# Six experts behind an attention: VectorE's and ScalarE's order written out by hand, the background work dealt into named slots, and the gating's column sums set behind the last group of a step

## The chip, the core and the metric

The kernel runs on one core of a Trainium2 chip. In the profile TensorE is PE (its weight loads PEld), VectorE is DVE, ScalarE is ACT, SyncE is SP, which issues the transfers here. Times are device microseconds (us) unless a unit stands beside them; a kernel's time is the median of its runs.

## The reference: what is computed

An attention with a complex decay per channel (4 batches, 8 heads, 768 positions, width 48 per head) yields 3072 tokens of 384 channels. They go through a mixture of eight experts, each two matrix products with a ReLU between; every token uses every expert, weighted by a gate matrix P that is normalised by rows and columns in turn, eight times.

```
x   = attention(q, k, v, a)                     # [3072, 384]
P   = exp(x @ w_gate - max)                     # [3072, 8]
for _ in range(8):
    P /= P.sum(1, keepdims=True) + 1e-9         # rows
    P /= P.sum(0, keepdims=True) + 1e-9         # columns
    P *= N / E
out = sum over e of P[:, e] * (relu(x @ w1[e]) @ w2[e])     # w1 384x1024, w2 1024x384
```

## The kernel before

**Stages.** `phase1` computes the attention and, beside it, experts 0 and 1, whose results go to DRAM (`ye_d`), as do the tokens (`x_d`). `phase2a` finishes these two experts, prepares the first weights, and does the first three normalising rounds (`HEAD` is 3 of `ITERS` 8). `phase2b`, the stage that the change edits, does experts 2 to 7 and the five other rounds.

**Steps of phase2b.** The 3072 tokens are four units `u` of 768. A step of the loop over `steps` is one unit with one pair of hidden blocks (2 x 128 of the 1024 hidden channels) of one expert. The steps run over two pairs of units (`su`), experts 2 to 7 (`e`), the two units of the pair (`ul`), and four pairs of blocks (`p`): 2 x 6 x 2 x 4 = 96 steps, eight of one expert in a row, called q = 0 to 7 below.

**One step on PE.** The hidden values of a step are four tiles of 128x384: c11, c12, c21, c22 (hidden block by half of the unit's tokens). The kernel makes them by a scheme of the Strassen kind from seven products P1 to P7 with eleven terms. A product's operands are sums of weight blocks (A, S) and of token blocks (B, T). Each operand is split into a high and a low part in fp32r, and each term is three matmuls (high x high, high x low, low x high: L785 to L787), so a step has 33. Two PSUM banks (tag `ph`) serve the products in turn: a product can start once the product before the last has been read. The second layer of a step is issued a step late, among the products of the next one: `l2(k)`, k = 0 to 5, calls `second` for one group of 128 tokens, six matmuls (L746 to L748) into the accumulator `po[k]`; 36 in a step.

**One step on the other engines.** ACT copies P1 and P5 out of PSUM as s1 and s5 (L800). DVE adds (L795): u2 = P6 + s1, u3 = P7 + u2, u4 = u2 + s5, c22 = u3 + s5, c11 = P2 + s1, c21 = P4 + u3, c12 = P3 + u4. Of each c, ACT makes the high part hh of its ReLU (L806), and DVE the remainder hl (L807).

**Background work**, done among the steps:

- Weights: `raw_w` (L648) loads the two weight matrices' blocks of a pair by one transfer of 768 KB, and `prep_w` makes five sums on DVE (L666), copies of the high parts on ACT (L668) and the remainders on DVE (L669) for the tiles wa (A blocks), wb (the sums) and wc (the second matrix).
- Tokens of the next unit: `load_x` (L607) issues the transfers and returns `jobs`: sums on DVE (tx, L623), high copies on ACT (L626) and remainders on DVE (L627) of T1 to T4. `l2` takes up to two jobs per group.
- Normalising: `rows` (five DVE instructions, L593 to L597, the last a partial sum `cs` over tiles), then `columns`: a small matmul by a matrix of ones that finishes the column sums (cp, L601), and four DVE instructions (L602 to L605).
- Ends of an expert: six evictions per unit, by ACT where e = 2 (L753), else by DVE into `oa` (L755), and for e = 7 the transfer to `out` (L757). `start` (L726 to L734), for e = 3, fetches experts 0 and 1 from `ye_d`, scales `oa` by P, and adds them.

**What sets the order.** A schedule is written out by hand for PE alone (L108): PE's order is the order in which the code issues its matmuls. The order on DVE, ACT and SP is chosen by a scheduler with its own estimates of durations, within the program's dependencies; so a background instruction in `l2(1)` may land elsewhere on DVE.

## Time and profile before

| what | value |
|---|---|
| median of three runs | 1807.05 (1807.03 to 1812.23) |
| the profiled execution's own time | 1808.5 |
| its span on the core | 1806.7 |
| its mean granted clock of TensorE | 0.993 |
| second-layer matmuls, lines L746, L747, L748, 1152 each | 385.3, 385.2 and 385.7 busy, 334 to 335 ns each |
| weight loads from DRAM, 48 of 768 KB | 4.2 from issue to landing (median) |

The page's first part gives each engine's busy time and its share of the span. Successive matmuls overlap, so the interval from one's start to the next's is shorter than the 335 ns that one is shown busy. A share is a mean over stages with different limits, so the timeline, the table by stretches and the waits are read for `phase2b` by itself. In a row of the timeline stand the start, the duration, the engine, the line, the operation, output and inputs; a bracket at its end gives idle time before it and what ended this. A line's number is one of the kernel above.

### The profile page before, as it was taken

The page shows a single profiled execution, that of the slowest core. Times are in us where ns is not written, and L with a number is a line of the kernel's source. Part 1 is how long each engine was busy: PE and PEld are TensorE (multiplying, and loading weights), DVE is VectorE, ACT ScalarE, POOL GpSimd, SP SyncE. Part 2 cuts the span into 40 slices and gives each one's busy share as a digit, 9 for nine tenths or more (in the row PEclk, how much of TensorE's full clock was granted, in tenths as well). Part 3 has the DMA queues.
Part 4 walks back from the last instruction along what each step waited for, and adds up shares of the span by engine and source line. Part 5 has one row for each costly group of instructions (what it writes and reads, how often), then busy time and mean ns, then how long its engine had stood idle before and what let it go on. Part 6 is the DMA issues. An engine that isn't in the chain of part 4 may idle for free. (4 is left out here: it accounts for less than half of the span.)

```text
span 1806.7 us, 30538 instructions
## 1 busy us (share of the span) xinstructions
PE 1756.0 (97%) x12024; PEld 1725.3 (95%) x12024; DVE 1361.6 (75%) x3060; ACT 730.1 (40%) x1597; POOL 6.4 (0%) x15
## 2 busy tenths in 40 slices
PE   5989999999999999999999999999999999999998
PEld 3889999999999999999999999999999999999998
DVE  7898999999973778867675757577876767675754
ACT  7544544554543533433343324243433333342421
POOL 1000000000000000000000000000000000000000
PEclk9999999999999999999999999999999999999999
DMA  6333334343442322201010201231220101010100
GB/s 213 94 118 118 109 119 121 119 125 118 120 106 96 122 70 79 97 18 53 18 53 1 71 1 53 84 114 48 88 71 20 52 18 53 11 61 1 53 27 28
DMA packets 120632, 132.83 MB, mean 74 GB/s; under 512 B 9632, under 2 KB 100512, under 8 KB 120480
## 3 DMA queue, kind: packets, MB, share of 16 engines
q1 hardware_dynamic: 119680, 130.41, 23.3%
q8 instruction: 96, 1.57, 0.4%
q14 instruction: 56, 0.46, 0.1%
q10 hardware_dynamic: 800, 0.39, 0.1%
HBM read 88.22 MB, written 23.59 MB: 62 GB/s over the span
## 5 line engine op out<-in xcount | busy, mean ns | idle before, releaser
L748 PE MATMUL po<-wc,hl 128*128 128x384 f32 x1152 | 385.7, 335 | 3.0 <-DVE hl L807 3.0
L746 PE MATMUL po<-wc,hh 128*128 128x384 f32 x1152 | 385.3, 334 | 0.0
L747 PE MATMUL po<-wc,hh 128*128 128x384 f32 x1152 | 385.2, 334 | 0.0
L806 ACT ACTIVATE hh<-c 128x384 fp32r<-128x384 f32 x384 | 200.9, 524 | 322.4 <-DVE c L795 321.1
L807 DVE SCALAR_TENSOR_TENSOR hl<-c,hh 128x384 fp32r<-128x384 f32 x384 | 212.2, 553 | 65.9 <-ACT hh L806 58.0
L748 PEld LDWEIGHTS po<-wc,hl 128*128 128x128 f32 x1152 | 216.5, 188 | 4.3 <-DVE hl L807 4.2
L746 PEld LDWEIGHTS po<-wc,hh 128*128 128x128 f32 x1152 | 216.5, 188 | 0.2 <-ACT hh L806 0.2
L747 PEld LDWEIGHTS po<-wc,hh 128*128 128x128 f32 x1152 | 216.5, 188 | 0.0
L800 ACT ACTIVATE s<-P 128x384 f32<-128x384 f32 x192 | 94.1, 490 | 278.6 <-PE P L787 278.5
L180 PE MATMUL ph<-xl,w 128*128 128x256 f32 x576 | 162.8, 283 | 3.5 <-DVE xl L531 3.4
L185 ACT ACTIVATE hh<-ph 128x256 fp32r<-128x256 f32 x192 | 73.3, 382 | 226.8 <-PE ph L181 226.1
L181 PE MATMUL ph<-xh,w 128*128 128x256 f32 x576 | 162.4, 282 | 0.0
L179 PE MATMUL ph<-xh,w 128*128 128x256 f32 x576 | 162.1, 281 | 0.0
L785 PE MATMUL P<-B,wa 128*128 128x384 f32 x480 | 160.4, 334 | 0.5 <-DVE c L795 0.5
L787 PE MATMUL P<-B,wa 128*128 128x384 f32 x480 | 160.4, 334 | 0.0
L786 PE MATMUL P<-B,wa 128*128 128x384 f32 x480 | 160.4, 334 | 0.0
L158 PE MATMUL po<-w,hh 128*128 128x384 f32 x384 | 136.3, 355 | 0.0
L795 DVE TENSOR_TENSOR c<-P,u 128x384 f32<-128x384 f32 x192 | 106.4, 554 | 31.7 <-PE P L787 30.6
L795 DVE TENSOR_TENSOR u<-u,s 128x384 f32<-128x384 f32 x96 | 53.5, 557 | 100.7 <-ACT s L800 100.3
L159 PE MATMUL po<-w,hh 128*128 128x384 f32 x384 | 129.3, 337 | 0.0
L160 PE MATMUL po<-w,hl 128*128 128x384 f32 x384 | 129.3, 337 | 0.0
L180 PEld LDWEIGHTS ph<-xl,w 128*128 128x128 f32 x576 | 108.9, 189 | 4.4 <-DVE xl L531 4.4
(188 smaller groups left out, 3606.0 us busy)
## 6 DMA issues: line engine op xcount, KB each, us to landing
raw<-in_w_dram SPq DMA_DIRECT2D x48, 768.0 KB, 4.2
qs<-z SPq DMA_DIRECT2D x144, 64.5 KB, 2.6
qk<-in_aqk_dram SPq DMA_DIRECT2D x12, 768.0 KB, 4.7
ks<-kh SPq DMA_DIRECT2D x144, 64.0 KB, 2.6
ye_d<-yst SPq DMA_DIRECT2D x48, 192.0 KB, 1.9
y<-ye_d SPq DMA_DIRECT2D x48, 192.0 KB, 2.4
z<-in_aqk_dram SPq DMA_DIRECT2D x11, 768.0 KB, 7.2
B<-x_d SPq DMA_DIRECT2D x40, 192.0 KB, 3.3
```

What stands on the lines that cost most here:

```text
L179: nc.tensor.matmul(ph, w[:, 0, cs], xh[:, ct, :], start=(ct == 0), stop=False)
L180: nc.tensor.matmul(ph, w[:, 0, cs], xl[:, ct, :], start=False, stop=False)
L181: nc.tensor.matmul(ph, w[:, 1, cs], xh[:, ct, :], start=False, stop=(ct == NCT - 1))
L746: nc.tensor.matmul(po[k], hh[:, s], w2[:, 0, i], start=first, stop=False)
L747: nc.tensor.matmul(po[k], hh[:, s], w2[:, 1, i], start=False, stop=False)
L748: nc.tensor.matmul(po[k], hl[:, s], w2[:, 0, i], start=False, stop=last)
L785: nc.tensor.matmul(ps, t[:, 0, k], x[:, 0], start=first, stop=False)
L786: nc.tensor.matmul(ps, t[:, 0, k], x[:, 1], start=False, stop=False)
L787: nc.tensor.matmul(ps, t[:, 1, k], x[:, 0], start=False, stop=last)
L795: V.tensor_tensor(o, a, b, ALU.add)
L806: A.activation(hh, c, AF.Relu)
L807: V.scalar_tensor_tensor(hl, c, 0.0, hh.bitcast(F32), ALU.max, ALU.subtract)
```

## The change

**Order.** The loop body of `phase2b` becomes a function `step`, run under a manual schedule for DVE and ACT too. Their order is now the order of the code; SP's is still the scheduler's. The first stage and `phase2a` keep the old rule.

**Slots.** A step has six slots, `fill(0)` to `fill(5)`, at fixed places among its instructions, which DVE mostly fills; and `post[0]` and `post[1]`, for copies on ACT. Which background work goes to which slot is set by the step's number n and by q. `deal(k)` runs up to k jobs of `load_x`.

**Weights.** One load of 768 KB becomes two of 384 KB, `raw0` and `raw1` (the two matrices), each issued behind the last reader of its forerunner. `prep_w` becomes `prep_w1` (sums, wa, wb) and `prep_w2` (wc). They run at q = 1, 5, 6, 7 and q = 0, 1, 6, 7, where `prep_w` was called at q = 0 and 5 to 7. `prep_w` itself, still called twice in `phase2a`, makes its copies ahead of its remainders, wb first. Of four preparations issued ahead of step 1 (two in `phase2a`, two in step 0), the third and fourth move to steps 1 and 2.

**PE.** In a step each group `l2(k)` stands one product earlier: P1, l2(0), P6, l2(1), P7, l2(2), P5, l2(3), P2, P4, l2(4), P3, l2(5), where before the sequence was P1, P6, l2(0), P7, l2(1), P5, l2(2), P2, l2(3), P4, l2(4), P3, l2(5).

**Normalising.** `sink` holds steps 4 to 8, where steps 1 to 5 did it. `rows` is in slot 2, `columns` behind `l2(5)`, where they were in `l2(1)` and `l2(4)`.

**Scaling `oa` by P** (e = 2's results) moves from DVE to ACT: for the first two units 12 instructions of their own in steps 10 and 11, for the other two within the eviction itself. The evictions and the adding of experts 0 and 1 (`mixin`) have slots, and the fetch of these two stays ahead by a step.

The core of the diff:

```diff
+        return [
+            tt(t[0], f("B11", 0), f("B11", 1), ALU.add),
+            tt(t[1], t[1], t[4], ALU.add),
+            both(tt(t[0], t[1], t[0]), hi("T1", t[0])),
+            tt(t[2], f("B22", 0), f("B22", 1), ALU.add),
+            both(tt(t[3], t[2], t[0]), hi("T2", t[3])),
+            lo("T1", t[0]),
+            both(tt(t[1], t[2], t[1]), hi("T3", t[1])),
+            lo("T2", t[3]),
+            tt(t[2], f("B21", 0), f("B21", 1), ALU.add),
+            both(tt(t[2], t[2], t[3]), hi("T4", t[2])),
+            lo("T3", t[1]),
+            lo("T4", t[2]),
+        ]
...
+        r = self.raw[j, n] = self.wr.tile([128, 2, C], F32, tag=f"raw{j}", name=f"raw{j}_{n}")
+        self.nc.sync.dma_start(r, src[:, :, j * C:j * C + C])
...
+        def sums():
+            for o, a, b, op in ((0, A21, A22, ALU.add), (1, s[:, 0], A11, ALU.subtract), (2, A11, A21, ALU.subtract), (3, A12, s[:, 1], ALU.subtract), (4, A13, A23, ALU.subtract)):
+                V.tensor_tensor(s[:, o], a, b, op)
+
+        def hi(q):
+            t, k, src = parts[q]
+            return lambda: A.activation(t[:, 0, k], src, AF.Copy)
+
+        def lo(q):
+            t, k, src = parts[q]
+
+            def run():
+                V.tensor_tensor(t[:, 1, k], src, t[:, 0, k].bitcast(F32), ALU.subtract)
+                if q == 1:
+                    self.raw_w(0)
+            return run
+
+        return sums, [hi(q) for q in range(3)], [lo(q) for q in range(3)]
...
+        def lo():
+            V.tensor_tensor(w2[:, 1], raw, w2[:, 0].bitcast(F32), ALU.subtract)
+            self.raw_w(1)
+
+        return lambda: A.activation(w2[:, 0], raw, AF.Copy), lo
...
-                self.raw_w()
+                self.raw_w(0)
+                self.raw_w(1)
                 self.prep_w()
...
+        sink = range(npair, npair + ITERS - HEAD)
...
+            if e == 2:
+                oa[tt] = self.xa.tile([128, C], F32, tag=f"oa{u % SU}_{k}", name=f"oa{tt}")
+                if u < SU:
+                    A.activation(oa[tt], po[k], AF.Copy)
+                else:
+                    A.activation(oa[tt], po[k], AF.Copy, scale=self.P[:, tt, 2:3])
+            else:
+                V.scalar_tensor_tensor(oa[tt], po[k], self.P[:, tt, e:e + 1], oa[tt], ALU.mult, ALU.add)
...
+            def out(k):
+                if done:
+                    slots[(2, 2, 2, 3, 4, 5)[k]].append(lambda: evict(prev, k))
+
+            for k in range(2 * NS):
+                out(k)
+            w2 = q in (0, 6, 7) and n > 0
+            w1 = q in (1, 5, 6, 7) or n == 2
+            if w2 and n > npair and self.nprep[1] < self.nprep[0]:
+                hi, lo = self.prep_w2()
+                post[0].append(hi)
+                slots[1].append(lo)
+            if w1 and self.nprep[0] < len(self.todo):
+                sums, his, los = self.prep_w1()
+                slots[0].append(sums)
+                post[0].extend([his[2], his[0], his[1]])
+                slots[2].extend([los[2], los[0], los[1]])
+                if q in (1, 2):
+                    hi, lo = self.prep_w2()
+                    post[1].append(hi)
+                    slots[3].append(lo)
+            if n in sink:
+                slots[2].append(self.rows)
+            if su == 0 and n == 2 or su and e == 2 and ul == 0 and p == 2:
+                slots[2].append(lambda: deal(3))
+            if e == 2 and ul == 0 and p == 3:
+                slots[0].append(lambda: deal(2))
+                slots[1].append(lambda: deal(1))
+                slots[2].append(lambda: deal(4))
+                slots[3].append(lambda: deal(1))
+                slots[4].append(lambda: deal(1))
+            if su and e == 2 and ul == 0 and p == 2:
+                slots[1].append(lambda: deal(1))
+                slots[3].append(lambda: deal(1))
+            if e == E - 1 and q >= 5:
+                slots[3].append(lambda: deal(1))
+                slots[4].append(lambda: deal(2))
+                slots[5].append(lambda: deal(1))
+            tiles = [(su * SU + k // (2 * NS), k % (2 * NS)) for k in range(4 * NS)]
+            if su == 0 and e == 3 and q in (2, 3):
+                for k in range(2 * NS):
+                    tt = tile_of(q - 2, k)
+                    post[0].append(lambda o=oa[tt], tt=tt: A.activation(o, o, AF.Copy, scale=self.P[:, tt, 2:3]))
+            if 3 <= e < 6 and q in (1, 2):
+                k = (e - 3) * 4 + (q - 1) * 2
+                fetch(*tiles[k])
+                fetch(*tiles[k + 1])
+            if 3 <= e < 6 and q in (2, 3):
+                k = (e - 3) * 4 + (q - 2) * 2
+                slots[2].append(lambda: mixin(*tiles[k]))
+                slots[4].append(lambda: mixin(*tiles[k + 1]))
...
-                if p > 1 or n == 0 or su and e == 2:
-                    for _ in range(min(2, len(jobs))):
-                        jobs.pop(0)()
-                if k == 1 and 0 < n <= ITERS - it:
-                    self.rows()
-                if k == 4 and 0 < n <= ITERS - it:
-                    self.columns(self.psA.tile([128, E], F32, tag="ph", name=f"cp{it + n - 1}"))
 
             s1 = copy("s1", prod("P1", ("A11", "B11")))
+            fill(0)
+            for g in post[0]:
+                g()
+            l2(0)
             u2 = add("u2", prod("P6", ("S2", "T2")), s1)
-            l2(0)
+            l2(1)
+            fill(1)
             u3 = add("u3", prod("P7", ("S3", "T3")), u2)
-            l2(1)
+            l2(2)
+            fill(2)
             s5 = copy("s5", prod("P5", ("S1", "T1"), ("A23", "B32")))
             u4 = add("u4", u2, s5)
             c22 = add("c22", u3, s5)
-            l2(2)
+            h11 = high(1, 1, c22)
+            l2(3)
             c11 = add("c11", prod("P2", ("A12", "B21"), ("A13", "B31")), s1)
-            relu(1, 1, c22)
-            relu(0, 0, c11)
-            l2(3)
+            h00 = high(0, 0, c11)
+            low(1, 1, c22, h11)
             c21 = add("c21", prod("P4", ("A22", "T4"), ("A23", "B31")), u3)
-            relu(1, 0, c21)
+            h10 = high(1, 0, c21)
+            low(0, 0, c11, h00)
+            low(1, 0, c21, h10)
+            for g in post[1]:
+                g()
             l2(4)
+            fill(3)
             c12 = add("c12", prod("P3", ("S4", "B22"), ("S5", "B32")), u4)
-            relu(0, 1, c12)
+            h01 = high(0, 1, c12)
+            fill(4)
+            low(0, 1, c12, h01)
             l2(5)
-            if n == 0:
-                self.prep_w()
-                self.prep_w()
-            if prev is not None and prev[2] == SU - 1:
-                self.prep_w()
-            if e == 3:
-                a = p * 2 if ul == 0 else 8 + p
-                for k in range(a, a + 2 - ul):
-                    start(su * SU + k // (2 * NS), k % (2 * NS))
+            if n in sink:
+                self.columns(self.psA.tile([128, E], F32, tag="ph", name=f"cp{n}"))
+            fill(5)
+
+        with tc.manual_schedule(engines={mybir.EngineType.DVE, mybir.EngineType.Activation}):
...
+            for n, st in enumerate(steps):
+                su, e, ul, p = st
+                if e == 2 and ul == 0 and p == 0:
+                    jobs.extend(self.load_x(xb, 1, su * SU + 1))
+                if e == E - 1 and ul == 1 and p == 0 and su + 1 < SU:
+                    jobs.extend(self.load_x(self.xa, 0, su * SU + 2))
+                step(n, st, steps[n - 1] if n else None)
+            for k in range(2 * NS):
+                second(steps[-1], k)
+                evict(steps[-1], k)
```

Three places in the new order beside the old. First PE at the start of step 1 (P1_1 and P6_1 are products of step 1, po2_0_0 the first group's accumulator, hh and hl the hidden values of step 0). Before:

```order
L785 MATMUL P1_1_8800<-B11_0_8152,wa1_8530 128x384
L786 MATMUL P1_1_8800<-B11_0_8152,wa1_8530 128x384
L787 MATMUL P1_1_8800<-B11_0_8152,wa1_8530 128x384
L785 MATMUL P6_1_8806<-T2_0_8158,wb1_8531 128x384
L786 MATMUL P6_1_8806<-T2_0_8158,wb1_8531 128x384
L787 MATMUL P6_1_8806<-T2_0_8158,wb1_8531 128x384
L746 MATMUL po2_0_0_8812<-wc0_8513,hh00_0_8706 128x384
L747 MATMUL po2_0_0_8812<-wc0_8513,hh00_0_8706 128x384
L748 MATMUL po2_0_0_8812<-wc0_8513,hl00_0_8707 128x384
L746 MATMUL po2_0_0_8812<-wc0_8513,hh10_0_8719 128x384
L747 MATMUL po2_0_0_8812<-wc0_8513,hh10_0_8719 128x384
L748 MATMUL po2_0_0_8812<-wc0_8513,hl10_0_8720 128x384
```

And now:

```order
L894 MATMUL P1_1_8774<-B11_0_8152,wa1_8534 128x384
L895 MATMUL P1_1_8774<-B11_0_8152,wa1_8534 128x384
L896 MATMUL P1_1_8774<-B11_0_8152,wa1_8534 128x384
L798 MATMUL po2_0_0_8788<-wc0_8528,hh00_0_8738 128x384
L799 MATMUL po2_0_0_8788<-wc0_8528,hh00_0_8738 128x384
L800 MATMUL po2_0_0_8788<-wc0_8528,hl00_0_8753 128x384
L798 MATMUL po2_0_0_8788<-wc0_8528,hh10_0_8751 128x384
L799 MATMUL po2_0_0_8788<-wc0_8528,hh10_0_8751 128x384
L800 MATMUL po2_0_0_8788<-wc0_8528,hl10_0_8755 128x384
L894 MATMUL P6_1_8795<-T2_0_8158,wb1_8535 128x384
L895 MATMUL P6_1_8795<-T2_0_8158,wb1_8535 128x384
L896 MATMUL P6_1_8795<-T2_0_8158,wb1_8535 128x384
```

The second-layer group stands between P1 and P6, where it stood behind both.

Second, DVE at the start of step 0 (sum3, wa3, wb3, wc3 are the fourth weight preparation, rs, cs and P_90 the normalising). Before:

```order
L669 TENSOR_TENSOR wa3_8756<-raw3_8753,wa3_8756 128x384
L666 TENSOR_TENSOR sum3_8755<-sum3_8755,raw3_8753 128x128
L669 TENSOR_TENSOR wa3_8756<-raw3_8753,wa3_8756 128x256
L594 TENSOR_SCALAR rs_8344<-rs_8344 128x24
L666 TENSOR_TENSOR sum3_8755<-raw3_8753,sum3_8755 128x128
L595 RECIPROCAL rs_8344<-rs_8344 128x24
L596 TENSOR_TENSOR P_90<-P_90,rs_8344 128x192
L597 TENSOR_REDUCE cs_8345<-P_90 128x8
L669 TENSOR_TENSOR wb3_8757<-sum3_8755,wb3_8757 128x640
L795 TENSOR_TENSOR u2_0_8672<-P6_0_8668,s1_0_8666 128x384
L669 TENSOR_TENSOR wc3_8758<-raw3_8753,wc3_8758 128x768
L795 TENSOR_TENSOR u3_0_8678<-P7_0_8674,u2_0_8672 128x384
```

And now:

```order
L904 TENSOR_TENSOR u2_0_8706<-P6_0_8702,s1_0_8700 128x384
L904 TENSOR_TENSOR u3_0_8712<-P7_0_8708,u2_0_8706 128x384
L904 TENSOR_TENSOR u4_0_8723<-u2_0_8706,s5_0_8721 128x384
L904 TENSOR_TENSOR c22_0_8725<-u3_0_8712,s5_0_8721 128x384
L904 TENSOR_TENSOR c11_0_8736<-P2_0_8729,s1_0_8700 128x384
L919 SCALAR_TENSOR_TENSOR hl11_0_8740<-c22_0_8725,hh11_0_8727 128x384
L904 TENSOR_TENSOR c21_0_8749<-P4_0_8742,u3_0_8712 128x384
L919 SCALAR_TENSOR_TENSOR hl00_0_8753<-c11_0_8736,hh00_0_8738 128x384
L919 SCALAR_TENSOR_TENSOR hl10_0_8755<-c21_0_8749,hh10_0_8751 128x384
```

Preparation and rows are gone from between and ahead of the step's sums, and u2, u3, u4, c22 and c11 follow one another.

Third, DVE in step 49, where the third unit gives way to the fourth (tx and T_3 are `load_x`'s jobs of unit 3). Before:

```order
L795 TENSOR_TENSOR u3_49_14952<-P7_49_14948,u2_49_14937 128x384
L623 TENSOR_TENSOR tx1_3_14911<-tx1_3_14911,tx4_3_14914 128x384
L623 TENSOR_TENSOR tx0_3_14910<-tx1_3_14911,tx0_3_14910 128x384
L623 TENSOR_TENSOR tx3_3_14913<-tx2_3_14912,tx0_3_14910 128x384
L623 TENSOR_TENSOR tx1_3_14911<-tx2_3_14912,tx1_3_14911 128x384
L795 TENSOR_TENSOR u4_49_14972<-u2_49_14937,s5_49_14970 128x384
L795 TENSOR_TENSOR c22_49_14974<-u3_49_14952,s5_49_14970 128x384
L627 TENSOR_TENSOR T1_3_14906<-tx0_3_14910,T1_3_14906 128x384
L666 TENSOR_TENSOR sum28_15517<-raw28_14899 128x128 x3
L623 TENSOR_TENSOR tx2_3_14912<-B21_3_14902 128x384
L627 TENSOR_TENSOR T2_3_14907<-tx3_3_14913,T2_3_14907 128x384
L795 TENSOR_TENSOR c11_49_14992<-P2_49_14985,s1_49_14931 128x384
```

And now:

```order
L904 TENSOR_TENSOR u3_49_15008<-P7_49_15004,u2_49_14995 128x384
L688 TENSOR_TENSOR wb27_14968<-sum27_14966,wb27_14968 128x640
L688 TENSOR_TENSOR wa27_14967<-raw0_27_14732,wa27_14967 128x384
L688 TENSOR_TENSOR wa27_14967<-raw0_27_14732,wa27_14967 128x256
L904 TENSOR_TENSOR u4_49_15031<-u2_49_14995,s5_49_15029 128x384
L904 TENSOR_TENSOR c22_49_15033<-u3_49_15008,s5_49_15029 128x384
L904 TENSOR_TENSOR c11_49_15051<-P2_49_15044,s1_49_14974 128x384
L919 SCALAR_TENSOR_TENSOR hl11_49_15055<-c22_49_15033,hh11_49_15035 128x384
```

Ahead of c11 stood ten background instructions in two places (sum28 is three); now three weight remainders stand between u3 and u4, and none between c22 and c11.

More of the change, by code (lines that the diff above doesn't have):

```diff
@@ L652, in prep_w, with tt, hi, lo @@
-    def prep_w(self):
-        nc, V, A = self.nc, self.nc.vector, self.nc.scalar
-        n = self.nprep
+        def tt(o, a, b, op=ALU.subtract):
+            return lambda: V.tensor_tensor(o, a, b, op)
+        def hi(nm, r):
+            return lambda: A.activation(X[nm][:, 0], r, AF.Copy)
+        def lo(nm, r):
+            return lambda: V.tensor_tensor(X[nm][:, 1], r, f(nm, 0), ALU.subtract)
+        def both(*fs):
+            def run():
+                for g in fs:
+                    g()
+            return run
@@ L675, in phase2a, with prep_w @@
+    def prep_w(self):
+        sums, his, los = self.prep_w1()
+        sums()
+        for q in (2, 0, 1):
+            his[q]()
+        for q in (2, 0, 1):
+            los[q]()
+        for g in self.prep_w2():
+            g()
     def phase2a(self, c2):
@@ L711, in phase2b @@
         tc, nc = self.tc, self.nc
+        V, A = nc.vector, nc.scalar
         self.hp = c2.enter_context(tc.tile_pool(name="hp2", bufs=2))
@@ L714, in phase2b @@
         psD = c2.enter_context(tc.tile_pool(name="psD", bufs=2, space=bass.MemoryType.PSUM))
-        steps = [(su, e, ul, p) for su in range(SU) for e in range(2, E) for ul in range(SU) for p in range(NF // 2)]
         npair = NF // 2
-        po, oa, H = {}, {}, {}
+        NE = E - 2
+        steps = [(su, e, ul, p) for su in range(SU) for e in range(2, E) for ul in range(SU) for p in range(npair)]
+        po, oa, H, Y, jobs = {}, {}, {}, {}, []
+        free = [(pool, tag) for pool, tag in ((self.psC, "po0"), (self.psC, "po1"), (self.psC, "po2"), (psD, "po"), (psD, "po"))]
+        sink = range(npair, npair + ITERS - HEAD)
         def acc(e, u, k):
@@ L739, in second @@
             h, w2 = H[st]
+            w2 = w2[1]
             if p == 0:
@@ L759, in phase2b, with evict @@
-        V, A = nc.vector, nc.scalar
-        jobs, free = [], [(pool, tag) for pool, tag in ((self.psC, "po0"), (self.psC, "po1"), (self.psC, "po2"), (psD, "po"), (psD, "po"))]
-        it = HEAD
-        for n, st in enumerate(steps + [None]):
-            prev = steps[n - 1] if n else None
-            if st is None:
-                for k in range(2 * NS):
-                    second(prev, k)
-                break
+        def evict(st, k):
             su, e, ul, p = st
             u = su * SU + ul
-            if e == 2 and ul == 0 and p == 1:
-                jobs = self.load_x(xb, 1, u + 1)
-            if e == E - 1 and ul == 1 and p == 1 and su + 1 < SU:
-                jobs = self.load_x(self.xa, 0, u + 1)
-            W, w2 = self.W[(su * (E - 2) + e - 2) * npair + p]
-            X = self.X[u]
-            h = {}
-            H[st] = (h, w2)
+            tt = tile_of(u, k)
+            if e == 2:
[6 more added lines that the diff above has]
+                V.scalar_tensor_tensor(oa[tt], po[k], self.P[:, tt, e:e + 1], oa[tt], ALU.mult, ALU.add)
+            if e == E - 1:
+                nc.sync.dma_start(self.out[tt * CH:tt * CH + CH, :], oa[tt])
@@ new lines, in deal, with step, fill @@
+        def deal(k):
+            for _ in range(min(k, len(jobs))):
+                jobs.pop(0)()
+        def step(n, st, prev):
+            su, e, ul, p = st
+            u = su * SU + ul
+            q = ul * npair + p
+            done = prev is not None and prev[3] == npair - 1
+            h = {}
+            H[st] = (h, self.W[(su * NE + e - 2) * npair + p])
+            W, X = H[st][1][0], self.X[u]
+            slots = {k: [] for k in range(6)}
+            post = {k: [] for k in range(3)}
+            def out(k):
[10 more added lines that the diff above has]
+            if w1 and self.nprep[0] < len(self.todo):
+                sums, his, los = self.prep_w1()
+                slots[0].append(sums)
[35 more added lines that the diff above has]
+                slots[4].append(lambda: mixin(*tiles[k + 1]))
+            def fill(k):
+                for g in slots[k]:
+                    g()
@@ L781, in prod @@
                 ps = pool.tile([128, TH], F32, tag=tag, name=f"{nm}_{n}")
-                for q, (wn, xn) in enumerate(terms):
+                for i, (wn, xn) in enumerate(terms):
                     (t, k), x = W[wn], X[xn]
-                    first, last = q == 0, q == len(terms) - 1
+                    first, last = i == 0, i == len(terms) - 1
                     nc.tensor.matmul(ps, t[:, 0, k], x[:, 0], start=first, stop=False)
```

95 lines of the change are left out of this document (38 added, 57 removed).

## The prediction

> Times are microseconds. Step n is pass n of the loop over `steps` (0 to 95); a time "in a step" counts from the issue of its first matmul of P1. q is its place among the eight steps of one expert.
>
> **What bounds the kernel now.** First the busy table of the page: TensorE (PE) is the only full engine.
>
> ```profile
> PE 1756.0 (97%) x12024; PEld 1725.3 (95%) x12024; DVE 1361.6 (75%) x3060; ACT 730.1 (40%) x1597; POOL 6.4 (0%) x15
> ```
>
> The change touches the stage of six experts, so I measure that stage against its own matmuls. From the timeline of PE: the stage's first matmul, its 39th, and its last one.
>
> ```profile
> 632.63 0.33 PE L785 MATMUL P<-B,wa 128*128 128x384 f32 x1
> ...
> 639.22 0.34 PE L787 MATMUL P<-T,wb 128*128 128x384 f32 x1
> ...
> 1800.57 0.34 PE L748 MATMUL po<-wc,hl 128*128 128x384 f32 x1
> ```
>
> Between the first two lie 38 issues: 6.59 / 38 = 0.1734 a matmul. A step has 33 product matmuls (eleven terms of three) and 36 of the second layer; 96 x 69 = 6624 take 1148.6. The stage lasted 1800.57 + 0.17 - 632.63 = 1168.1, so 19.5 are lost. Where, the table by stretches shows (columns: length, then busy time of PE, weight load, DVE, ACT, POOL, then granted clock):
>
> ```profile
> 642.00:644.00 2.00, 1.39 (x6) 1.37 (x6) 0.57 (x2) 0.25 (x1) 0.00 (x0) 0.74 1.13 345
> 644.00:646.00 2.00, 2.00 (x8) 2.00 (x7) 1.71 (x6) 0.00 (x0) 0.00 (x0) 0.50 0.73 205
> ...
> 740.00:764.00 24.00, 22.16 (x126) 21.50 (x125) 18.69 (x40) 7.44 (x15) 0.00 (x0) 1.00 0.34 109
> 764.00:788.00 24.00, 24.00 (x140) 24.00 (x140) 13.58 (x27) 6.26 (x13) 0.00 (x0) 1.00 0.00 1
> ...
> 1172.00:1196.00 24.00, 22.54 (x128) 21.72 (x127) 20.61 (x45) 10.86 (x22) 0.00 (x0) 1.00 0.20 67
> 1220.00:1244.00 24.00, 21.18 (x117) 19.89 (x117) 21.30 (x46) 9.03 (x17) 0.00 (x0) 1.00 0.28 91
> 1316.00:1340.00 24.00, 21.96 (x124) 21.01 (x123) 22.55 (x52) 9.71 (x21) 0.00 (x0) 1.00 0.31 99
> ```
>
> Most stretches are full (24.00). PE starves only where VectorE (DVE) is crowded: the start, the normalising steps, the change of units near 1172 to 1340. The waits of that stage by releaser (total, times, longest):
>
> ```profile
> PEld P L785 <- DVE c L795: 7.6, 9, 2.0
> PEld P L785 <- ACT s L800: 4.4, 4, 1.5
> PEld po L748 <- DVE hl L807: 4.2, 4, 1.5
> PEld P L785 <- DVE u L795: 1.4, 2, 1.0
> ```
>
> They sum to 17.6 of the 19.5; the halved clock after 642.6 adds 0.5 + 1.0 + 0.2 = 1.7. No DMA stands there. One case, step 49 of the old order:
>
> ```profile
> 1236.76 0.55 DVE L627 TENSOR_TENSOR T<-tx,T 128x384 fp32r<-128x384 f32 x1
> 1237.22 0.55 DVE L795 TENSOR_TENSOR c<-P,s 128x384 f32<-128x384 f32 x1
> 1237.83 0.45 PE L785 MATMUL P<-B,wb 128*128 128x384 f32 x1 [0.30 <-DVE c L795]
> ```
>
> A background subtraction (T) stands directly ahead of c11, whose reading of P2 releases the bank that P3 waits for. The order on DVE is what stops PE here, and that order is what the change edits.
>
> **The change, part by part.** DVE prices come from back-to-back stretches, where the gap from start to start is the cost:
>
> ```profile
> 1218.53 0.89 DVE L669 TENSOR_TENSOR wa<-raw,wa 128x384 fp32r<-128x384 f32 x2
> 1219.34 0.61 DVE L755 SCALAR_TENSOR_TENSOR oa<-po,P,oa 128x384 f32<-128x384 f32 x1
> 1219.87 0.28 DVE L666 TENSOR_TENSOR sum<-raw,sum 128x128 f32<-128x128 f32 x1
> 1220.07 0.55 DVE L623 TENSOR_TENSOR tx<-B 128x384 f32<-128x384 f32 x1
> ...
> 1222.00 0.81 DVE L669 TENSOR_TENSOR wb<-sum,wb 128x640 fp32r<-128x640 f32 x1
> 1222.73 0.55 DVE L795 TENSOR_TENSOR c<-P,s 128x384 f32<-128x384 f32 x1
> ...
> 1228.73 0.95 DVE L669 TENSOR_TENSOR wc<-raw,wc 128x768 fp32r<-128x768 f32 x1
> 1229.59 0.55 DVE L795 TENSOR_TENSOR u<-P,s 128x384 f32<-128x384 f32 x1
> ```
>
> So: both wa remainders 0.81, wb 0.73, wc 0.86, an eviction 0.53, a sum 0.20 (five: 1.05), any other 128x384 operation 0.47 (1236.76 to 1237.22), its result after 0.55. Hand-overs, from the end of the program:
>
> ```profile
> 1792.17 0.53 ACT L806 ACTIVATE hh<-c 128x384 fp32r<-128x384 f32 x1 [1.55 <-DVE c L795]
> 1792.73 0.56 DVE L807 SCALAR_TENSOR_TENSOR hl<-c,hh 128x384 fp32r<-128x384 f32 x1 [0.59 <-ACT hh L806]
> ...
> 1795.37 0.33 PE L748 MATMUL po<-wc,hl 128*128 128x384 f32 x1
> 1795.74 0.62 DVE L755 SCALAR_TENSOR_TENSOR oa<-po,P,oa 128x384 f32<-128x384 f32 x1 [0.37 <-PE po L748]
> ```
>
> ACT to DVE 0.03; PE to DVE 0.20 after the matmul's 0.17 slot; DVE to PE 0.06 (1237.77 to 1237.83).
>
> *PE's order.* New step: P1 at 0, then second-layer groups and products in turn: P6 1.56, P7 3.12, P5 4.68, P2 6.76, P4 7.80, P3 9.88, next P1 11.96. Two product banks alternate, so each product waits for the reading of the one two before. With DVE and ACT free: s1 is done at 1.2 (P7 needs it at 3.12), u2 2.83 (P5, 4.68), u3 4.39 (P2, 6.76), s5 6.41 (P4, 7.80), c11 8.55 (P3, 9.88), c12 11.67 (next P6, 13.52). The old order put P6 directly behind P1, so c12 had until 12.48 and s1 until 2.08: margins of 0.75 and 0.9 grow to 1.8 and 1.9. In exchange P4 now follows P2 directly: margins of s5 and c11 fall from about 2.4 to 1.3. I cost the swap at nothing; its cover is that 1.3.
>
> *Slots in plain steps.* After u3 (issued until 4.31) DVE is free till s5 brings u4 at 6.44: 2.1 that hold slot 2, and P3 waits only from about 4.0 of it. Weight remainders need 0.73 + 0.81 = 1.54, three evictions 1.6, two mixins 1.06. Slot 0 holds the sums from 0.8 to 2.35, ahead of u2 (due by 4.1); slot 1 a wc remainder ahead of u3, 2.75 to 3.62. Slots 3 to 5 put off the start of c12 to 11.8 at most (done 12.4, due 13.5). ACT's weight copies run between s1 and s5, 1.2 to 5.9; three of them, each no longer than the first row below, fit. So the 88 steps other than 0 to 3 and 5 to 8 come out with no wait, the unit changes (45 to 51, one to four `load_x` jobs a slot) too.
>
> ```profile
> L668 ACT ACTIVATE wc<-raw 128x768 fp32r<-128x768 f32 x45 | 38.1, 848 | 36.5 <-PE P L787 25.1 <-PE po L748 11.4
> raw<-in_w_dram SPq DMA_DIRECT2D x48, 768.0 KB, 4.2
> ```
>
> The second row, from the page's DMA issues, is a whole weight load, 4.2 from issue to landing. The halves are issued behind their last readers (about 5.9 and 3.6 in a step) and are wanted at the next step's start or later, at least 6 ahead: hidden.
>
> *Start.* The stops there in the old order:
>
> ```profile
> 641.23 0.44 PE L748 MATMUL po<-wc,hl 128*128 128x384 f32 x1 [1.15 <-DVE hl L807]
> ...
> 642.63 0.44 PE L748 MATMUL po<-wc,hl 128*128 128x384 f32 x1 [0.61 <-DVE hl L807]
> ```
>
> Two of four weight preparations and the first row pass leave DVE here, and step 0 becomes a bare chain: s5 from 2.8, u4, c22 and c11 to 4.8, hl11 at 5.4, c21 and hl00 to 6.4, hl10 done at 7.08. The second layer wants hl10 at 5.72 + 0.52 + 5 x 0.173 = 7.11. Both stops and the slow clock behind them go; I leave 0.1.
>
> *Step 2.* Slot 2 carries the remainders and three of `load_x`'s jobs, 4.31 to 7.35, and ACT's T1 copy stands ahead of s5: s5 is done at 8.35 instead of 6.41, P4 (7.80) waits 0.6. After a wait the next issue is 0.1 late too (1237.83 to the following matmul 0.28): 0.7.
>
> *Normalising, steps 4 to 8.* One row pass and one matmul for the column sum:
>
> ```profile
> 618.14 0.35 DVE L593 TENSOR_REDUCE rs<-P 128x24 f32<-128x192 f32 x1
> ...
> 619.62 0.53 DVE L597 TENSOR_REDUCE cs<-P 128x8 f32<-128x192 f32 x1
> ...
> 652.13 0.34 PE L748 MATMUL po<-wc,hl 128*128 128x384 f32 x1
> 652.30 0.28 PE L601 MATMUL cp<-cs,ones 128*128 128x8 f32 x2
> ...
> 652.74 0.34 PE L786 MATMUL P<-B,wb 128*128 128x384 f32 x1
> ```
>
> The rows cost 1.75 (to 620.1, less an hl between); the column sum 0.27 of PE (0.61 less two slots), five times 1.35, as before. Here cp takes a product bank, so the next P1 needs c12 by 12.06. Steps 5 to 7 put 1.54 + 1.75 = 3.3 into slot 2, u4 starts at 7.6 to 8.1, and the lateness is handed on: c12 done at 11.84, 12.09, 12.31 in steps 5, 6, 7. PE waits 0, 0.03, 0.25; with restarts 0.4.
>
> *Scaling by P* moves from DVE to ACT, in steps 10 and 11 six times at most 0.5 behind s1, done by 4.2, before s5 at 5.9: nothing. *Before 632* the third preparation leaves DVE ahead of cp2, which waited:
>
> ```profile
> 629.18 0.39 PE L601 MATMUL cp<-cs,ones 128*128 128x8 f32 x2 [0.33 <-DVE cs L597]
> ```
>
> That wait goes; a wb copy now stands ahead of the exponential on ACT and may make cp0 as late. Net zero, 0.4 either way.
>
> **The sum.** Left of 19.5: 0.1 + 0.7 + 0.4 + 1.35 = 2.55; saved 16.95, call it 17. The profiled execution took 1808.5 (span 1806.7), 1.45 above the median 1807.05 of the three runs: 1791.5 for such an execution, 1790 for the median. Bounds of what I cannot see: all waits gone gives 1807.05 - 18.1 = 1788.9, 0.3 less if cp0 is on time; small waits of 0.1 in one step of three give 3 more, 1793.
>
> A granted clock of 0.50 followed gaps of 1.15 and 0.6 within 3. The Trainium skill (TensorE: Matmul & The Clock Gate, The HAM clock gate) wants an idle window of about 3.4 for that; by it those gaps were not the cause, the dip could stay, and the sum would be 1791.7. The row shows a drop with no gap that long, so I keep 1790.
>
> **The rivals.**
>
> (a) *Crowded slots cost more.* If slot 2 of steps 2, 3 and 5 to 8 runs a microsecond longer than its parts, each stops P4, P3 or P1 by about 1: 6 more, 1796. For it: DVE was busy 22.55 of 24 at 1316 and PE waited; against: the parts above are measured in such crowds.
>
> (b) *DVE cannot overlap neighbours.* If it waits out each result, 0.55 instead of 0.47, a step of 28 instructions (steps 5 to 7) grows by 2.3 and stops P1 by about 2, three times: 1796. Against: the rows start 0.47 behind an instruction of 0.55. This is how the Trainium skill (VectorE: DVE Perf Modes, The DRAIN you can't avoid) puts it, the next instruction starting only when the pipe is empty; the trace disagrees.
>
> (c) *Late data move the waits.* If the `tx` and half-weight loads, not the order, set the stops at 1172 to 1244, those 2.3 + 4.1 (24 less 21.72, less 19.89) stay: 1796. For it: SP's queue is one line, and a load behind an output waits with it; against: the releasers of PE name DVE and ACT only.
>
> (d) *Slower.* The thinner margin of c11, 1.3, is exceeded in every step: P4 straight behind P2 leaves P3 waiting. It starts from 1.27 of added delay; 0.18 beyond that in each of 96 steps eats the 17, and 0.3 gives 1790 + 29 = 1819. For it: DVE and ACT hold to one order now, so any late item holds c11 up; against: in plain steps slot 2 is empty, and nothing measured above is 1.27 late.
>
> **How the numbers follow.** Forecast 0.78 (own range 1788 to 1793.5), (a) 0.09, (b) 0.02, (c) 0.06, (d) 0.03, no effect at all 0.02. The range 1787.8 to 1796 takes in the forecast and the near side of (a) to (c). About 0.3% (5.4) can be told from no change here: forecast and (a) to (c) lie below 1801.6, so faster 0.95, same 0.02, slower 0.03.
>
> **What would show it.** In the new profile: PE's waits in this stage near 1 in all, not 17.6; stretches near 640, 740, 1230 and 1320 at 24.00; granted clock 1.00 throughout the stage; a wait of P4 on s5 of about 0.6 in step 2 and of P1 on c12 of about 0.25 in step 7; the stage 1151 long. Waits of P3 on c11 in plain steps would prove (d), of DVE on DMA (c).

## The result

| | before | changed |
|---|---|---|
| median, first chip (4 runs each) | 1807.78 (1807.03 to 1812.23) | 1790.80 (1790.25 to 1792.06) |
| ratio, first chip | | 0.9896 (0.9884 to 0.9908) |
| profiled execution: time, span | 1808.5, 1806.7 | 1792.06, 1790.3 |
| first matmul of the stage, its length | 632.63, 1168.1 | 633.42, 1150.8 |
| median, another chip | 1811.74 (7 runs) | 1791.24 (4 runs) |
| ratio, the other chip | | 0.9884 (0.9867 to 0.9900) |

Behind a median stand its lowest and highest run, behind a ratio its 95% interval. The change is faster by 17.0 on the first chip, 1.0%; 1790.0 was forecast. The stage became 17.35 shorter, and it began 0.8 later. The busy table of the changed kernel, from its page:

```profile
PE 1751.3 (98%) x12024; PEld 1725.8 (96%) x12024; DVE 1366.8 (76%) x3036; ACT 733.6 (41%) x1609; POOL 6.4 (0%) x15
```

DVE does as much as before (1361.6), so the gain is not work taken away. The table by stretches, for the same stretches as before:

```profile
642.00:644.00 2.00, 2.00 (x13) 2.00 (x13) 1.86 (x8) 0.61 (x2) 0.00 (x0) 1.00 1.00 290
644.00:646.00 2.00, 2.00 (x14) 2.00 (x13) 2.00 (x5) 1.34 (x4) 0.00 (x0) 1.00 0.42 119
740.00:764.00 24.00, 24.00 (x141) 24.00 (x140) 16.67 (x32) 12.68 (x25) 0.00 (x0) 1.00 0.22 65
...
1172.00:1196.00 24.00, 24.00 (x140) 24.00 (x139) 21.80 (x49) 11.80 (x24) 0.00 (x0) 1.00 0.24 70
1220.00:1244.00 24.00, 24.00 (x140) 24.00 (x140) 17.96 (x35) 8.29 (x16) 0.00 (x0) 1.00 0.13 38
1316.00:1340.00 24.00, 24.00 (x140) 24.00 (x140) 16.41 (x31) 6.80 (x13) 0.00 (x0) 1.00 0.22 66
```

Every stretch that had holes is full, and the clock behind the start is 1.00. Between 1172 and 1196 DVE is busier than it was (21.80 for 20.61), and PE waits for nothing. All waits of PE's weight loads in the stage, by releaser (total, times, longest), come to 1.2, where the rows shown of before made 17.6:

```profile
PEld P L894 <- ACT s L909: 0.8, 1, 0.8
...
PEld P L894 <- DVE c L904: 0.2, 1, 0.2
PEld po L800 <- DVE hl L919: 0.2, 1, 0.2
```

The first is P4 of step 2, the second P1 of step 8 behind c12, the third step 1's second layer. The timeline of PE shows the first of them:

```profile
658.97 0.34 PE L896 MATMUL P<-B,wa 128*128 128x384 f32 x1
659.80 0.45 PE L894 MATMUL P<-T,wa 128*128 128x384 f32 x1 [0.49 <-ACT s L909]
660.08 0.34 PE L895 MATMUL P<-T,wa 128*128 128x384 f32 x1
```

The prediction left one thing out: what VectorE and ScalarE themselves waited for in this stage. Of the kernel before, the waits for transfers:

```profile
DVE sum L666 <- DMA raw<-in_w_dram: 34.1, 34, 1.7
DVE tx L623 <- DMA out_dram<-oa: 1.4, 2, 0.9
DVE tx L623 <- DMA tx<-x_d: 1.0, 1, 1.0
ACT wa L668 <- DMA raw<-in_w_dram: 67.9, 34, 4.5
```

Old DVE stood still for 36.5 in all because the next instruction in its line was background work whose load had not come (1.4 of it waited for an output transfer to be done with the tile). In the changed kernel the same list holds no transfer at all. A case that ended in a stop of PE, the timeline of the kernel before:

```profile
1217.25 0.29 DVE L666 TENSOR_TENSOR sum<-raw 128x128 f32<-128x128 f32 x1 [1.64 <-DMA raw<-in_w_dram]
1217.46 0.55 DVE L795 TENSOR_TENSOR u<-P,u 128x384 f32<-128x384 f32 x1
...
1223.34 0.45 PE L785 MATMUL P<-B,wb 128*128 128x384 f32 x1 [0.58 <-DVE c L795]
```

DVE idles 1.64 at the head of its line and is busy without a break from there; u3 and all behind it come late, and 6 us on PE waits 0.58 for c11, which starts at 1222.73. The releaser named at PE is DVE; what held DVE was a weight load.

### The profile page after: what moved, and what is told of

It is laid out like the page before. It is cut to its first block, busy times and chain, and to the rows that moved or that the text cites. A ratio compares the mean times of both kernels' runs of the same rounds, so it can differ in the third digit from the quotient of the medians.

```text
span 1790.3 us, 30678 instructions
## 1 busy us (share of the span) xinstructions
PE 1751.3 (98%) x12024; PEld 1725.8 (96%) x12024; DVE 1366.8 (76%) x3036; ACT 733.6 (41%) x1609; POOL 6.4 (0%) x15
## 4 chain that ended last, share of the span: by engine, by line
PE 91%; DVE 6%; DMA 1%; ACT 1%; issue 1%; SPq 0%; ACTq 0%; DVEq 0%
PE po L800 11%; PE po L799 11%; PE po L798 11%; PE P L894 10%; PE P L896 10%; PE P L895 10%; PE po L158 4%; PE ph L180 4%; PE ph L181 4%; PE ph L179 3%; PE po L159 3%; PE po L160 3%; PE sp L474 2%; PE y L491 2%; PE U L469 1%; DMA wr<-in_w_dram 1%
## 5 line engine op out<-in xcount | busy, mean ns | idle before, releaser
L909 ACT ACTIVATE s<-P 128x384 f32<-128x384 f32 x192 | 94.1, 490 | 317.8 <-PE P L896 317.8
L187 DVE TENSOR_TENSOR hl<-hf,hh 128x256 fp32r<-128x256 f32 x192 | 81.0, 423 | 48.3 <-ACT hf L186 46.9
```

## The experiments

Each kernel is compared with the kernel before on its own chip (where that took 1811.5 to 1811.7), and profiles with each other by the length of the stage: from the issue of its first matmul of P1 to its last matmul's issue and 0.17. The kernel before has 1168.1, the change 1150.8. The stretch ahead of it is measured from a small matmul at L583, ahead of the normalising, to the stage's first matmul: 23.81 before, 23.51 in the change. Theory A at the outset was the prediction's: a stop comes where background work stands ahead of the reader of a product bank on DVE.

**The order left to the scheduler.**

```diff
-        with tc.manual_schedule(engines={mybir.EngineType.DVE, mybir.EngineType.Activation}):
+        if True:
```

> The changed kernel, with VectorE's and ScalarE's order left to the scheduler again (PE's order, slots and placement in the code as changed). Theory A (stops come from background work that stands ahead of a bank's reader; who writes the order is no matter in itself): in the scheduler's order steps 5 to 8 keep rows between u3 and u4 as by hand, step 0 has c12 and two tx ahead of hl10 (done about 7.9 where 7.1 is needed, 0.8), steps 1 and 45 put tx and T remainders ahead of u3 or c11 (about 0.5 each): 2 to 4 more than the change, 1793 to 1795. Rival (the hand-written order carries the gain): the scheduler's order brings the stops back, 1800 or more.

Measured: 1810.0, ratio 0.9993 (0.9983 to 1.0002): nothing is left of the gain. The profiled execution was the fastest of ten (1804.5); its stage took 1163.7, 12.9 more than the change, and the stretch ahead of it 25.78, 2.3 more. The median lies another 5.5 higher; the nine other executions list a mean granted clock of 0.990 to 0.992 for the 0.994 of this one, but no trace shows what they lost. Its waits, of PE's weight loads and of DVE:

```profile
PEld P L894 <- DVE c L904: 7.4, 5, 2.8
PEld po L800 <- DVE hl L919: 6.6, 6, 2.3
...
DVE sum L678 <- DMA raw<-in_w_dram: 39.2, 41, 4.1
```

And its timeline at one stop:

```profile
1219.15 0.69 DVE L678 TENSOR_TENSOR sum<-raw 128x128 f32<-128x128 f32 x3 [4.06 <-DMA raw<-in_w_dram]
...
1222.63 0.55 DVE L904 TENSOR_TENSOR c<-P,s 128x384 f32<-128x384 f32 x1
...
1223.23 0.44 PE L894 MATMUL P<-B,wb 128*128 128x384 f32 x1 [2.50 <-DVE c L904]
```

The rival was right, and my 2 to 4 was wrong by its own method: I added up DVE's durations in the scheduler's order and left out that DVE stands still where a load is late (4.06 here, 1.71 for a token load at 640.2 in step 0, from which the stop of 1.94 at 641.75 follows). The half loads are in this kernel too, and it still waits 41 times for them: the smaller loads alone do not cure it. The hand-written order with whole loads was not run, so whether it needs the halves stays open. Theory A becomes A': a stop comes where background work stands ahead of a bank's reader, by its own duration and by the time that its data are late.

**VectorE's order alone by hand.**

```diff
-        with tc.manual_schedule(engines={mybir.EngineType.DVE, mybir.EngineType.Activation}):
+        with tc.manual_schedule(engines={mybir.EngineType.DVE}):
```

> The changed kernel with only VectorE's order by hand; ScalarE's is the scheduler's. Theory A' (VectorE's order carries the gain, after the run that left both to the scheduler lost 13 of the stage's 17): the scheduler puts T1's copy of step 2 behind s5 (0.7 less) and in step 9 sixteen copies ahead of s5 (12 x 0.5 + 2.4 behind s1 at 1.2, s5 done at 10.2 where P4 needs it at 7.8: 2.5 more): the stage about 1152.5. Rival (ScalarE's order carries it): 1160 or more.

Measured: 1795.3, ratio 0.9916 (0.9900 to 0.9933); stage 1154.05. Of the 12.9 that the scheduler costs in the stage, ScalarE's part alone is 3.3, so DVE's order carries the other 9.6; the 2.3 ahead of the stage are gone too (23.51). Both forecast places are there: no wait in step 2, and P4 of step 9 waits for s5 behind sixteen copies, 2.65 between its issue and the one before, 2.5 late as worked out. Not foreseen were two waits of P1 for c12, 0.79 each, in the normalising steps, where ScalarE now puts a wc copy ahead of hh11 and hh00. DVE waits for no transfer in this run either.

**PE's old order in the changed kernel** (the third eviction goes to slot 3, as its group ends later).

```diff
-            l2(0)
             u2 = add("u2", prod("P6", ("S2", "T2")), s1)
-            l2(1)
+            l2(0)
             fill(1)
             u3 = add("u3", prod("P7", ("S3", "T3")), u2)
-            l2(2)
+            l2(1)
...
-            l2(3)
+            l2(2)
...
+            l2(3)
             c21 = add("c21", prod("P4", ("A22", "T4"), ("A23", "B31")), u3)
```

> The changed kernel with PE's old order within a step (P6 directly behind P1; each group one product later), and the third eviction in slot 3 since its group ends later. Theory A (PE's new order is worth nothing by itself, the prediction's cost of zero): by the same timetable c12 is done at 11.85 where P6 needs it at 12.48, s1 at 1.2 where P7 needs it at 2.08, and only steps at an expert's start, with two evictions ahead of c12, come 0.1 late: 1791, at most 1793. In the normalising steps P1 needs c12 by 12.23, margin 0.38 less what slot 3 adds. Rival (the wider margins of c12 and s1 carry the gain): most of the 17 come back, 1800 or more.

Measured: 1796.7, ratio 0.9918 (0.9901 to 0.9934); stage 1156.1, 5.3 more. Between the two theories: PE's order carries under a third, but not nothing. Its waits:

```profile
PEld P L894 <- DVE cs L602: 2.0, 5, 0.4
PEld P L894 <- ACT s L909: 1.2, 2, 1.0
PEld P L894 <- DVE c L904: 0.8, 1, 0.8
```

I had left out two readers. In the normalising steps P6 follows P1 directly and needs the bank of cp, which DVE reads only behind hl01: five times 0.4. And at the start s1 of step 1 waits on ScalarE for hh01 of step 0, so P7 waits 0.67. The new order puts six matmuls between. The rest is a wait of P6 for c12 in step 3, the third row, and delays of about 0.1 at experts' starts, which were expected.

**PE's new order in the kernel before.**

```diff
-            u2 = add("u2", prod("P6", ("S2", "T2")), s1)
             l2(0)
-            u3 = add("u3", prod("P7", ("S3", "T3")), u2)
+            u2 = add("u2", prod("P6", ("S2", "T2")), s1)
             l2(1)
+            u3 = add("u3", prod("P7", ("S3", "T3")), u2)
+            l2(2)
...
-            l2(2)
+            l2(3)
...
-            l2(3)
             c21 = add("c21", prod("P4", ("A22", "T4"), ("A23", "B31")), u3)
```

> The kernel before with only PE's order within a step changed to the new one; VectorE and ScalarE stay with the scheduler, preparations, rows and transfers as before. Theory A: c12 and s1 gain 1.1 of margin, s5 and c11 lose as much, and background work still stands ahead of c11 and c22 (step 49: six pieces between u3 and u4, five between c22 and c11, so c11 is done at about 10.4 where 9.88 is needed); a part of the 19.5 goes, most stays: 1798 to 1806. Rival (PE's order carries the gain): 1791 to 1793.

Measured: 1811.2, ratio 1.0000 (0.9990 to 1.0009): no change; the stage of the profiled execution took 1172.7, if anything longer than before's 1168.1. PE's new order is worth nothing without the other engines' order, as A says, though no part of the 19.5 went, where I had expected some.

**The old code's own order, fixed by hand, without slots.**

```diff
-                self.phase2b(c2)
+                with tc.manual_schedule(engines={mybir.EngineType.DVE, mybir.EngineType.Activation}):
+                    self.phase2b(c2)
```

> The kernel before with VectorE's and ScalarE's order in the six-expert stage fixed as its code stands, with no slots: a whole preparation follows the last remainder of its step. Theory A (it matters where background work stands, not that the order is fixed): in each of 46 preparations the four copies stand on ScalarE ahead of the next s1. The sums end at about 13.9, the copies at 15.5, s1 at 16.0, where P7 needs the bank at 11.96 + 2.08 = 14.04: PE waits 2.0 each time, 46 x 2.0 = 92 more than a stage without stops, 1788 + 92 = 1880 (1850 to 1920). Rival (a fixed order by itself removes the stops): 1795 or less.

Measured, in one execution: 1935.2, stage 1295.4, 145 longer than the changed one's. By releaser:

```profile
PE P L786 <- ACT s L801: 94.1, 45, 12.5
...
PE P L786 <- DVE u L796: 15.5, 14, 2.5
```

The sign and the place are A's: P7 waits for s1 in 45 steps, 12.5 once and (94.1 - 12.5) / 44 = 1.85 else, for the 2.0 expected. The rest of the miss is the 12.5, step 0's two preparations in a row, the second of which waits 5.5 for its load (its wa copy, at 649.47), the waits for u, and the clock: 108 matmuls of this stage follow each other 0.32 apart instead of 0.173, which is 16 (mean granted clock 0.982). A fixed order by itself is thus far worse than the scheduler's; what the change brings is the order and the places together.

**Delay ahead of c11**, three and six additions per step.

```diff
             h11 = high(1, 1, c22)
+            for _ in range(6):
+                V.tensor_tensor(u4, u2, s5, ALU.add)
             l2(3)
```

> The changed kernel with three extra VectorE additions in every step, straight ahead of c11 (u4 written again with the same value): 3 x 0.47 = 1.41 of VectorE, of which 0.62 falls into idle time before P2 ends, so c11 is 0.79 later. Theory A (c11's margin to P3 is about 1.3): hidden in plain steps; steps 5 to 8, where the order is full, lose up to 1.4 each: the stage takes 1152 to 1157 instead of 1150.8. Rival (d) of the prediction (the thin margin is used up already): 0.79 lost in every step, 76 more, 1227.

> The same with six additions, 2.82 of VectorE, c11 2.20 later. Theory A: the excess over 1.3 stops P3 in each of 96 steps, about 0.9 and 0.1 for the restart: 1.0 x 96 = 96 more, the stage 1247 (1235 to 1260). If VectorE had slack to take it in, no change; if each addition costs its whole 0.47 on PE, 270 more. A granted clock of 0.5 behind such gaps of 1.0 would say that gaps of this length alone slow PE down.

Measured: stages of 1161.1 and 1334.1, one execution each (1803.2 and 1975.5). The timeline of a plain step with six:

```profile
911.42 0.56 DVE L904 TENSOR_TENSOR c<-u,s 128x384 f32<-128x384 f32 x1
911.89 3.52 DVE L942 TENSOR_TENSOR u<-u,s 128x384 f32<-128x384 f32 x6
915.33 0.55 DVE L904 TENSOR_TENSOR c<-P,s 128x384 f32<-128x384 f32 x1
...
915.93 0.44 PE L894 MATMUL P<-B,wb 128*128 128x384 f32 x1 [1.45 <-DVE c L904]
```

The six cost (915.33 - 911.89) / 6 = 0.573 each and not 0.47. Each writes the tile that the one before wrote; that this is the reason is likely, but no run varies it alone. With that price the theory's margin gives 6 x 0.573 - 0.62 - 1.27 = 1.55, and 0.1 for the restart: 1.65 a step. From one stopped P3 to the next (902.23 to 915.93) a step takes 13.70 for 11.96, 1.74 more; 96 x 1.74 = 167 of the 183, and the rest stands in the full steps and in the half clock behind five of them (last section). The waits of that kernel up to 1950 name c11 in 94 steps, and one more follows:

```profile
PEld P L894 <- DVE c L904: 172.0, 94, 2.9
```

Three of them, 1.65, leave plain steps without a stop: c11 is then 1.03 late, and 1.27 is not reached. So the margin of c11 to P3 lies where the prediction had it. The 10.3 that three additions cost all come from few places (eight waits for c, 7.6 in all, and steps 1 and 2), above all steps 2 to 7; the upper end that I gave was 6.2.

**The normalising back in steps 1 to 5.**

```diff
-        sink = range(npair, npair + ITERS - HEAD)
+        sink = range(1, 1 + ITERS - HEAD)
```

> The changed kernel with the normalising in steps 1 to 5 as before (rows in slot 2, columns behind the last group, all else as changed). Theory A: slot 2 of steps 1 to 3 now holds a preparation or load_x's jobs and rows. Step 2: T1's copy stands ahead of s5 and behind 4.7 of VectorE work, P4 waits about 2.4 instead of 0.8; step 3: T4's copy behind 3.7, P4 waits about 1; steps 6 and 7 give 0.3 back: the stage 2 to 3 longer than 1150.8. Rival (the place of the normalising carries the gain): 6 or more longer.

Measured: 1797.6, ratio 0.9928 (0.9911 to 0.9944); stage 1156.6, 5.8 longer, more than A and a little less than the rival's 6. Its waits:

```profile
PEld P L894 <- ACT s L909: 4.1, 2, 2.6
...
PEld P L894 <- DVE c L904: 2.8, 3, 1.5
```

The first row is P4 of steps 2 and 3, 2.4 and 1.3 late by their issues (2.4 and 1 expected). The second I had left out: with rows, preparation and jobs in one step, P1 behind the first three cp waits for c12. A third of the gain hangs on where the normalising stands, and by the mechanism of A'.

**The third and fourth preparation ahead of the stage.**

```diff
         more(len(todo))
+        self.prep_w()
+        self.prep_w()
...
-            w1 = q in (1, 5, 6, 7) or n == 2
+            w1 = q in (1, 5, 6, 7) and n > 1
```

> The changed kernel with the third and fourth weight preparation made ahead of the stage (in phase2a, where the scheduler deals them), instead of in steps 1 and 2. Theory A (what stood in the way at the old kernel's start was background work between step 0's own sums; preparations finished ahead of it cost the stage nothing): steps 0 and 1 keep their few tenths, and step 2 loses its stop, since nothing but two pieces and T1 stand in slot 2: stage 1150.0. Ahead of it 7 more of VectorE work stand among the rows: cp1 and cp2 come 0.3 to 0.6 late each, so the time is the same within 0.5. Rival (the place of these preparations carries the start's gain): stops and halved clock near the first 12 us of the stage, 3 to 5 more.

Measured: stage 1149.97, as forecast, with no wait in step 2 and none at the start beyond the tenths; time 1792.9, ratio 0.9898 (0.9881 to 0.9915), not told apart from the change beside it (1791.2), though not within the 0.5 expected either. Ahead of the stage the three cp wait 1.2 for their rows, and the stretch from L583 takes 24.91 for 23.51: the preparations cost 1.4 there and save 0.8 in the stage. The start's gain is not bound to these preparations being in steps 1 and 2. That it needs them out from between step 0's sums is read from the old trace; no run puts them back.

**Two mended versions, and the change once more.** The first moves T1's copy of step 2 behind s5 and spreads the normalising:

```diff
-        sink = range(npair, npair + ITERS - HEAD)
+        sink = (4, 5, 7, 8, 9)
...
+            if su == 0 and n == 2:
+                slots[2].append(lambda: deal(2))
+                slots[3].append(lambda: deal(1))
```

The second has `sink = (1, 2, 4, 5, 8)`, the same two lines for step 2, and the preparations ahead of the stage.

> The changed kernel once more, on the chip of the runs beside it. Theory: its stage is set by its order and takes 1150.8 again, within 0.3; what differs from run to run lies ahead of the stage. Were the stage's few stops chance, its length would move by a microsecond or more.

> The changed kernel with T1's difference and copy of step 2 in slot 3 instead of slot 2, and the normalising in steps 4, 5, 7, 8 and 9 instead of 4 to 8. Theory A: T1's copy stands behind s5, so P4 of step 2 does not wait (0.76 less); no three full steps in a row, so P1 of step 8 does not wait for c12 (0.29 less): stage 1149.7, the time about 1 below the control. If the stops are not set by these two places, the stage stays at 1150.8.

> The third and fourth preparation ahead of the stage, T1's copy of step 2 behind s5, and the normalising in steps 1, 2, 4, 5 and 8. Theory A: no stop is left but the five column sums' 0.22 and step 0's tenths: stage 1149.9 or less; ahead of the stage as in the run with the preparations moved, so the time within 1 of the control.

Measured: the change 1791.2 with a stage of 1150.74, so the stage repeats to 0.02 on another chip. The first mended version: 1791.2 (ratio 0.9887, 0.9870 to 0.9903), stage 1150.51 for the 1149.7 expected: both old stops are gone, and a new one is there, P1 of step 10 waiting 0.80 for c12, since step 9 now holds a preparation, the rows and wc:

```profile
747.74 0.28 PE L601 MATMUL cp<-cs,ones 128*128 128x8 f32 x2
748.82 0.44 PE L897 MATMUL P<-B,wa 128*128 128x384 f32 x1 [0.80 <-DVE c L907]
```

The second: 1791.6 (0.9889, 0.9873 to 0.9906), stage 1149.55, the shortest of all, behind a stretch from L583 of 25.08, 1.6 longer than in the change. Neither beats the change by an amount that the times can tell.

## Why the prediction was right, and what it did not see

**The sum.** Of 19.5 lost in the stage it left 2.55. Taken from PE's intervals beyond 0.1734, the change has 0.23 at the start of step 1 (0.1 forecast), 0.76 in step 2 (0.7: 0.83 and 0.28 between issues, the rows shown), and 1.5 at the five column sums (1.75: 0.22 each where nothing waits, for 0.27; and 0.1 and 0.3 of waits in the last two full steps, for 0.4 in all). That makes 2.5; 1150.8 less 1148.6 gives 2.2, the difference being the rounding of 0.1734 over 6624 matmuls. Every place named was the right one; that the sum is out by so little is in part luck, as 0.1 too little at the start and 0.25 too much at the column sums offset each other. The stage of 1151 came to 1150.8.

**Ahead of the stage** it counted nothing, 0.4 either way. cp2's wait of 0.33 is gone, as said; the stage nevertheless began 0.8 later. This is from before the code that changed: the small matmul at L583 was issued at 608.82 before and at 609.91 after, and between 607.3 and 610.9 in the runs above. Profiled executions differ there by up to 3.6, so the medians' 0.8 over the forecast lie within that spread.

**The bound.** "No DMA stands there" was read from PE's releasers alone, and is the step that fell short. DVE and ScalarE waited for loads in the old order, and the run with the scheduler's order shows that such waits end in PE's stops. The forecast held all the same, since in the hand-written order all of it is gone: sums stand a step behind their load, and DVE's list shows no transfer. It was right there for half a reason: that the half loads come in time was worked out, that late loads were part of what it removes was not seen. Rival (c), which feared late data, had the right resource and the wrong direction: the order cured them. How much of the old 17.6 came from late loads and how much from durations was not measured apart, but the old trace has both: at 1217 the load, and elsewhere DVE busy 9.93 of the 10 us from 632 to 642 and all of those from 737 to 748, without a wait for a transfer, ahead of the start's stops (1.15 and 0.61) and of the one for u at 747.58 (0.68). Late loads may also be why the kernel before took 1807.8 on one chip and 1811.7 on others while the change took 1790.8 and 1791.2; that is argued, not shown.

**PE's order** at nothing: right in the sum, since all was counted on the new timetable, but its value is 5.3 with the rest of the change and none without it. The cover named, 1.3 of c11, was measured by the doses.

**Rivals.** (a) and (b) need waits of 1 to 2 in each of steps 5 to 7; the longest there is 0.2. (d) needs the margin to be used up: 1.03 of delay in each plain step cost nothing, 2.82, which is 1.55 above the margin, cost 1.74. The last words of (b), that the trace disagrees, go too far: the section of the Trainium skill named there (VectorE: DVE Perf Modes, The DRAIN you can't avoid) lets an instruction that is not held start earlier, so starts 0.47 apart do not contradict it.

**The clock.** The granted clock of 0.50 near 644 went with the gaps of 1.15 and 0.61, as the rows had led me to take. The page that spoke against it (the Trainium skill, TensorE: Matmul & The Clock Gate, The HAM clock gate) could have left the dip in place; the trace shows 1.00 in all stretches there. By which rule the clock falls stays open (last section).

## What to carry to other kernels

On an engine that takes its instructions in order, background work costs what it lasts and also what its data are late: put it where both fit before the next reader of a scarce buffer, and follow a stop past the engine that released it to what that engine itself waited for. Work out for each product when its buffer must be read and how much fits ahead; the margin of c11 so found held to 0.1. In three runs that came out longer than forecast, a reader of a bank or a late load had been left out. An order by hand is worth only as much as its places: a fixed order without slots took 124 longer than the kernel before, and the slots without the order gained nothing.

## What the runs showed of the hardware that was not expected

**Clock.** The length of a gap alone does not tell whether the clock drops. In the kernel before with PE's new order, one gap of 3.12 (1238.92 to 1242.04) was followed by half clock until about 1248, and the drop came within the gap. The table by stretches of that kernel:

```profile
1238.00:1240.00 2.00, 1.26 (x8) 0.94 (x6) 2.00 (x7) 0.26 (x1) 0.00 (x0) 1.00 0.00 0
1240.00:1242.00 2.00, 0.00 (x0) 0.00 (x0) 2.00 (x6) 0.71 (x2) 0.00 (x0) 0.82 0.00 0
1242.00:1244.00 2.00, 1.96 (x6) 1.97 (x7) 2.00 (x6) 1.00 (x3) 0.00 (x0) 0.50 0.00 0
```

A mean of 0.82 over 1240 to 1242 puts the drop at 1241.28, 2.4 after the last issue. A gap of 2.62 in the same run (717.5 to 720.1), one of 2.83 with the scheduler's order (1220.4 to 1223.2), and the 1.78 of each plain step with six additions left it at 1.00. But in the crowded steps of that last run it fell five times, behind gaps of 2.43 to 2.94, and two gaps of one length went differently. From the last issue ahead of it (667.40 and 682.59) each of these P3 comes 2.94 later; behind the first the matmuls follow at the full rate, behind the second 0.32 apart:

```profile
670.34 0.44 PE L894 MATMUL P<-B,wb 128*128 128x384 f32 x1 [2.60 <-DVE c L904]
670.79 0.34 PE L896 MATMUL P<-B,wb 128*128 128x384 f32 x1
...
685.53 0.46 PE L894 MATMUL P<-B,wb 128*128 128x384 f32 x1 [2.60 <-DVE c L904]
686.11 0.52 PE L896 MATMUL P<-B,wb 128*128 128x384 f32 x1
```

The section of the Trainium skill named above (The HAM clock gate) has a free-running window of about 3.4; the slow stretch of 6.8 at 1242 (1241.3 to 1248.1, the matmuls 0.32 apart until 1247.96) fits two of them, and its chance phase fits that like gaps differ, but PE had not been idle for a whole window when the clock fell.

**VectorE.** Within the six additions above, each of which writes the tile its forerunner wrote, one starts (3.52 - 0.55) / 5 = 0.59 behind the other; additions that write another tile start 0.47 apart. A price by instruction count alone is off by a quarter in such a chain.
